# Sorted-block attention and a routed expert layer on one core: expert 0's last output as seven products, and part of a weight sum on another engine

## Chip, core and metric

The kernel runs on one core of a Trainium2 chip. The core has TensorE (matrix products into PSUM), VectorE, ScalarE and GpSimd (elementwise work), SyncE (it issues DMAs here) and 16 DMA engines. The metric is the device time of one execution in microseconds (us). Before the change the median of three runs is 681.45 us, and the runs lie between 679.47 and 681.47.

In the profile, PE is TensorE's matmuls, PEld its weight loads, DVE VectorE, ACT ScalarE, POOL GpSimd. L305 is line 305 of the kernel.

## What is computed

Four batches of 768 tokens with 8 heads of 64 go through a block attention whose keys and values are mixed by a small normalised matrix. Its output, 3072 tokens by 512, is the input x of an expert layer in which every expert works on every token, and a routing matrix P weighs the experts:

```python
logits = x @ w_gate                       # 3072 x 8
P = np.exp(logits - logits.max())
for _ in range(8):                        # eight rounds
    P /= P.sum(1, keepdims=True) + 1e-09  # rows: one token's experts
    P /= P.sum(0, keepdims=True) + 1e-09  # columns: one expert's tokens
    P *= N / E
for e in range(8):
    h = np.maximum(x @ w1[e], 0.0)        # 512 -> 1024
    out += P[:, e:e+1] * (h @ w2[e])      # 1024 -> 512
```

P is final only after eight rounds over all tokens, so it needs the attention of the last batch. The expert products do not need it; only the weighing of their outputs does.

## The kernel before

**Layout.** Matmul operands are bf16. `xtT` holds x transposed (features on partitions, 4 blocks of 128), `osbl` the output in f32 as 24 tiles of 128 tokens by 512, `glog` the logits and later P, 24 x 8 per partition. `w1t[e]` and `w2t[e]` are an expert's weights.

**Stages.** (1) Attention of batch 0, then of batches 1 to 3 with expert 0's products for batches 0 and 1 woven in. (2) Routing (`balance`, L440 to L476) with expert 0's products for batches 2 and 3 (`last_two`, L625), and, from the second of these batches on, with expert 1's first hidden units. (3) Experts 1 to 7, each for three groups of 1024 tokens: while one group's hidden layer is made (`hidden`, L481), the output of the group before it is made (`output7`, L559).

**Expert 0** uses plain products. `hidden0` makes 384 tokens' hidden layer in 8 steps of 4 matmuls of 384 columns (L305), with ReLU on ScalarE (L307). `output0` makes one tile of 128 tokens with 8 matmuls of 512 columns (L314) in two half steps; ScalarE then copies it to `osbl` (`keep`, L322) or, for batch 3, multiplies it by P's column as it copies (`keep_scaled`, L325), for which the rounds must be over.

**Experts 1 to 7** use seven products of half-size blocks in place of eight. That needs sums of operands: of x on VectorE (`sum_x`, L139, three plus one in place for each group of 1024 tokens), of w1 and w2 on GpSimd (`sum_w`, L338; `sum_w2`, L437) and of the hidden layer on GpSimd (`sum_h`, L557). A `hidden` unit has seven steps of two 512-column matmuls (L487). Between them ScalarE copies partial results out of PSUM (L507, L515, L520, L529) and VectorE adds them (L511, L523, L526, L533). Step 0's result is copied and then accumulated further in step 2, so step 2 waits for the copy. `output7` has seven steps of four 256-column matmuls (L574), each followed by a VectorE multiply-add into `osbl` (`gather`, L539). `scale0` (L609) multiplies expert 0's first 18 tiles by P on ScalarE.

**Routing.** `balance` is a chain. The maximum of the logits goes VectorE (L446), TensorE (L449), VectorE (L451), TensorE (L454), VectorE (L456), ScalarE's exponential (L457). Then eight rounds: VectorE's row steps (L464 to L468), a TensorE matmul that sums over partitions (L471), VectorE's column steps (L472 to L475). Each `yield` is a place at which the caller lets other work in.

**What sets the order.** Each engine runs its instructions in the order of its queue. A scheduler fills the queues from the order of the code and from what it takes to be ready, and moves ready work forward into gaps. `pin` (`keep_in_program_order`) holds an instruction behind all that was traced on its engine before it. The matmuls of stage 2 are pinned, as are the weight sums and weight loads of GpSimd. VectorE's and ScalarE's work and `sum_h` are not.

The last part of the kernel interleaves by hand: loop step `n` issues one step of `last_two`, from n = 28 one step of expert 1's first units, at the steps in `works` one of `sum_x`, and at 19 listed steps the next part of `balance`. At n = 40, behind the last round, a small GpSimd copy of P into `held` (L652) stands ahead of the eight sums for expert 1's w2, so they start only when routing is done. `load_w2(1)` is issued as soon as the attention's buffers are closed.

Of the kernel before, what the change touches and what calls it, by code (L numbers as in the profile page):

```python
# [13 lines left out]
F32 = mybir.dt.float32  # L14
BF16 = mybir.dt.bfloat16
AF = mybir.ActivationFunctionType
AX = mybir.AxisListType
ALU = mybir.AluOpType


def mkap(t, dims, off=0):
    return bass.AP(tensor=t.tensor, offset=t.offset + off, ap=dims)
# [3 lines left out]
def kernel(  # L26
# [11 lines left out]
    nc = tc.nc  # L38
    B, H, S, D = 4, 8, 768, 64
    NB, BL = 8, 96  # L40
    N, Dm, E, F = 3072, 512, 8, 1024
    NT = 24
    TB = S // 128
    scale = 1.0 / (D ** 0.5)
# [19 lines left out]
    pin = tc.keep_in_program_order  # L64
# [12 lines left out]
    w2t = {}  # L77
# [6 lines left out]
    def load_w2(e):  # L84
        w2t[e] = (wq if e else wcp).tile([128, 8, Dm], BF16, name="w2e")
        pin(nc.gpsimd.dma_start(out=w2t[e],
                                in_=moe_w2[e].rearrange("(fb k) f -> k fb f", k=128)))
# [18 lines left out]
    cs = pp.tile([32, 8], F32)  # L106
# [21 lines left out]
    osbl = xtp.tile([128, NT, Dm], F32)  # L128
    glog = xtp.tile([128, NT, E], F32)
# [168 lines left out]
            yield  # L298


    def hidden0(c0, hTs, hbank):
        for fb in range(8):
            hps = hbank()
            for kk in range(4):
                pin(nc.tensor.matmul(hps[:, 0:384], w1t[0][:, kk, fb * 128:(fb + 1) * 128],  # L305
                                     xtT[:, kk, c0:c0 + 384], start=(kk == 0), stop=(kk == 3)))
            nc.scalar.activation(out=hTs[:, fb, 0:384], in_=hps[:, 0:384], func=AF.Relu)  # L307
            yield

    def output0(c0, hTs, obank, done):  # L310
        for tt in range(3):
            oacc = obank()
            for fb in range(8):
                pin(nc.tensor.matmul(oacc, hTs[:, fb, tt * 128:(tt + 1) * 128],  # L314
                                     w2t[0][:, fb, :], start=(fb == 0), stop=(fb == 7)))
                if fb == 3:
                    yield
            done(c0 // 128 + tt, oacc)
            yield

    def keep(t, oacc):
        (nc.vector.tensor_copy if t < 12 else nc.scalar.copy)(osbl[:, t, :], oacc)  # L322

    def keep_scaled(t, oacc):
        nc.scalar.activation(out=osbl[:, t, :], in_=oacc, func=AF.Copy,  # L325
                             scale=glog[:, t, 0:1])

    wct = {}

# [11 lines left out]
    with tc.tile_pool(name="ps0", bufs=8, space=bass.MemoryType.PSUM,  # L341
# [14 lines left out]
        held = pp.tile([96, 2], BF16)  # L356
# [18 lines left out]
    with ExitStack() as c2:  # L375
# [13 lines left out]
        for bb, ns in ((1, (5, 3, 3, 5)), (2, (5, 3, 2, 4)), (3, (5, 4, 0, 5))):  # L389
# [11 lines left out]
            else:  # L401
                for _ in sums:
                    pass
                x0 = sum_x(0)
# [3 lines left out]
        for _ in ex:  # L408
# [6 lines left out]
    mpc, xcp, wq, wcq = late("mpc", 1), late("xcp", 2), late("wq", 2), late("wcq", 1)  # L415
    htp, fsp, hsp, w2q = late("htp", 2), late("fsp", 1), late("hsp", 3), late("w2q", 1)
# [2 lines left out]
                                        reuse_waits="tile"))  # L419
    op = ctx.enter_context(tc.tile_pool(name="op", bufs=3, space=bass.MemoryType.PSUM,  # L420
                                        reuse_waits="tile"))
    load_w2(1)

    def bank():
        return bk.tile([128, 512], F32, name="bk")

    w2s = {}

    def sum_w2(e):
        w2s[e] = (w2q.tile([128, 4, 4, Dm // 2], BF16, name="w2s") if e % 2 else  # L430
                  wcp.tile([128, 4, 4, Dm // 2], BF16, name="w2e"))
        for k in (0, 2):
            b11, b12 = (w2t[e][:, 4 + k:6 + k, d:d + 256] for d in (0, 256))
            b21, b22 = (w2t[e][:, k:k + 2, d:d + 256] for d in (0, 256))
            t1, t2, t3, t4 = (w2s[e][:, j, k:k + 2, :] for j in range(4))
            for a, b, c in ((b12, b11, t1), (b22, t1, t2), (b22, b12, t3), (b21, t2, t4)):
                pin(nc.gpsimd.tensor_tensor(out=c, in0=a, in1=b, op=ALU.subtract))  # L437
                yield

    def balance():  # L440
        onesc = mpc.tile([128, 128], F32)
        nc.vector.memset(onesc, 1.0)
        I128 = mpc.tile([128, 128], F32)
        nc.vector.tensor_copy(I128, Ibig)
        gm = mpc.tile([128, 1], F32)
        nc.vector.reduce_max(out=gm, in_=glog.rearrange("p t e -> p (t e)"), axis=AX.X)  # L446
        yield
        gmps = bank()[:, 0:128]
        pin(nc.tensor.matmul(gmps[0:1, :], gm, I128, start=True, stop=True))  # L449
        gm1 = mpc.tile([1, 1], F32)  # L450
        nc.vector.reduce_max(out=gm1, in_=gmps[0:1, :], axis=AX.X, negate=True)  # L451
        yield
        gnps = bank()[:, 0:128]
        pin(nc.tensor.matmul(gnps[:, 0:1], onesc[0:1, :], gm1, start=True, stop=True))  # L454
        gneg = mpc.tile([128, 1], F32)
        nc.vector.tensor_copy(gneg, gnps[:, 0:1])  # L456
        nc.scalar.activation(out=glog, in_=glog, func=AF.Exp, bias=gneg)  # L457

        rs2 = mpc.tile([128, NT], F32)
        cs2 = mpc.tile([128, E], F32)  # L460
        cs1 = mpc.tile([128, E], F32)
        yield
        for it in range(8):
            nc.vector.reduce_sum(out=rs2, in_=glog, axis=AX.X)  # L464
            nc.vector.tensor_scalar_add(rs2, rs2, 1e-9)
            nc.vector.reciprocal(out=rs2, in_=rs2)
            nc.vector.tensor_mul(glog, glog, mkap(rs2, [rs2.ap[0], rs2.ap[1], [0, E]]))
            nc.vector.reduce_sum(out=cs2, in_=glog.rearrange("p t e -> p e t"), axis=AX.X)  # L468
            yield
            csps = bank()[:, 0:128]  # L470
            pin(nc.tensor.matmul(csps[:, 0:E], onesc, cs2, start=True, stop=True))  # L471
            nc.vector.tensor_scalar(out=cs1, in0=csps[:, 0:E], scalar1=float(E) / N,  # L472
                                    scalar2=1e-9 * E / N, op0=ALU.mult, op1=ALU.add)
            nc.vector.reciprocal(out=cs1, in_=cs1)
            nc.vector.tensor_mul(glog, glog, mkap(cs1, [cs1.ap[0], [0, NT], cs1.ap[1]]))  # L475
            yield  # L476
# [60 lines left out]
    def gather(e, t, c, ps):  # L537
        o = osbl[:, t, c:c + ps.shape[-1]]
        nc.vector.scalar_tensor_tensor(out=o, in0=ps, scalar=glog[:, t, e:e + 1], in1=o,  # L539
                                       op0=ALU.mult, op1=ALU.add)  # L540
# [5 lines left out]
    hs = {}  # L546

    def sum_h(i, hT, f0=0, f1=4):

        if f0 == 0:  # L550
            hs[i] = hsp.tile([128, 3, 4, 128], BF16, name="hs")
        s1, s2, s4 = (hs[i][:, j, f0:f1] for j in range(3))
        a11, a21, a12, a22 = (hT[:, f + f0:f + f1, t + 128 * i:t + 128 * i + 128]
                              for f in (4, 0) for t in (0, 512))
        for a, b, o, c in ((a21, a22, ALU.add, s1), (s1, a11, ALU.subtract, s2),
                           (a12, s2, ALU.subtract, s4)):
            nc.gpsimd.tensor_tensor(out=c, in0=a, in1=b, op=o)  # L557
# [54 lines left out]
    def units(e, p, hT, hold=lambda ins: ins):  # L612
        for i in range(4):
            yield from hidden(e, p, i, hT, hold)

    queue = [sum_w2(1)]

    def sums(n):
        while n and queue:
            if next(queue[0], 0) is None:  # L620
                n -= 1
            else:
                queue.pop(0)

    def last_two():  # L625
        for bb, done in ((2, keep), (3, keep_scaled)):
            hT = htp.tile([128, 8, 1024], BF16, name="hT")
            halves = [(bb * S + c, hT[:, :, c:c + 384]) for c in (0, 384)]
            for c0, hTs in halves:
                yield from hidden0(c0, hTs, bank)  # L630
            for c0, hTs in halves:
                yield from output0(c0, hTs, lambda: op.tile([128, Dm], F32, name="oacc"), done)

    tail0, chain = last_two(), balance()
    x1, x2 = sum_x(1), sum_x(2)
    works = {0: x0, 10: x1, 14: x1, 19: x1, 23: x1, 41: x2, 43: x2, 46: x2, 48: x2}
    first = None
    for n in range(56):
        next(tail0)
        if n == 28:  # L640
            hT = htp.tile([128, 8, 1024], BF16, name="hT")
            first = units(1, 0, hT, pin)
        if first:
            next(first)
            if n == 28 + 21:
                sum_h(0, hT, 0, 3)
        if n in works:
            next(works[n], 0)
        if n in (0, 2, 4, 6, 8, 11, 13, 15, 17, 20, 22, 24, 26, 29, 31, 33, 35, 37, 39):
            next(chain)  # L650
        if n == 40:
            pin(nc.gpsimd.tensor_copy(held, glog[0:96, NT - 1, 0:2]))  # L652
            sums(8)

    hTs = {0: hT}

# [8 lines left out]
    for n in range(1, 3 * (E - 1) + 1):  # L665
        e, p, hT = 1 + (n - 1) // 3, (n - 1) % 3, hTs[n - 1]
        d = 2 + n // 3
# [49 lines left out]
```

## Time and profile before

| | |
|---|---|
| median of 3 runs | 681.45 us |
| profiled execution | 680.18 us, span 678.2 us |
| TensorE busy | 651.5 us, 96% of the span |
| VectorE, GpSimd, ScalarE busy | 545.2, 472.6, 298.5 us |
| routing: first row step to end of last column step | 120.31 to 153.35 us |
| TensorE's first matmul of `output7` | 172.51 us |

The profile's page has a row of busy tenths in 40 slices of the span (about 17 us each), the chain of work that ended last as shares of the span, and groups of instructions by line. The trace behind it gives every instruction with its start and length in us, then engine, line, operation and tiles; the number in brackets is how long the engine was idle before it and what ended that wait. Rows of waits give the engine and line that waited, what it waited for, the total, the times and the longest.

### The profile page before, as it was taken

Reading aid. Unit: us, or ns where it says so; the run is one execution under the profiler, and the core shown is the slowest. Engines: PE = TensorE matmul, PEld = TensorE weight load, DVE = VectorE, ACT = ScalarE, POOL = GpSimd, SP = SyncE. Lnnn points to the kernel's source line nnn. Section 1 sums busy time; section 2 is a strip of 40 time slices with the busy share of each in tenths; the row PEclk is TensorE's granted clock in tenths of the full one; section 3 lists DMA queues with packets and bytes.
Section 4 is the critical chain, followed back from the end, with each engine's and each line's share of the span. In section 5 each row is a group of like instructions: output and inputs, shape, how many; then the busy total and the mean of one; then the engine's idle time right before and its main releaser. Section 6 shows DMA issues by size and latency. Waiting matters only on the chain.

```text
span 678.2 us, 13166 instructions
## 1 busy us (share of the span) xinstructions
PE 651.5 (96%) x5033; PEld 436.5 (64%) x5108; DVE 545.2 (80%) x1154; ACT 298.5 (44%) x550; POOL 472.6 (70%) x499
## 2 busy tenths in 40 slices
PE   2999999999999999999999999999999999999996
PEld 1756766554566666666666666666666666666675
DVE  6727768763788888888988889888888889888896
ACT  3747764469533433334333343434333343333430
POOL 4542335007888988898997898689886999646745
PEclk9789999999999999999999999999999999999999
DMA  9898973100240330030303040034003120001223
GB/s 146 164 218 127 150 125 46 31 1 12 52 61 3 63 60 5 1 63 4 61 1 47 17 63 1 1 63 63 1 2 63 19 45 0 1 1 64 94 78 141
DMA packets 31903, 36.57 MB, mean 54 GB/s; under 512 B 2016, under 2 KB 24288, under 8 KB 31840
## 3 DMA queue, kind: packets, MB, share of 16 engines
q0 software_dynamic: 26400, 27.82, 25.9%
q1 hardware_dynamic: 5440, 7.90, 3.6%
q8 instruction: 40, 0.66, 0.4%
q14 instruction: 23, 0.19, 0.1%
HBM read 52.45 MB, written 6.29 MB: 87 GB/s over the span
## 4 chain that ended last, share of the span: by engine, by line
PE 72%; DVE 1%; issue 1%; POOL 1%; ACT 0%; DVEq 0%
PE oacc L574 37%; PE bk L487 34%; PE bk L574 1%; DVE osbl L539 1%; POOL hs L557 1%; DVE hT L523 0%; DVE hT L526 0%; ACT p L507 0%; DVEq L539 0%
## 5 line engine op out<-in xcount | busy, mean ns | idle before, releaser
L539 DVE SCALAR_TENSOR_TENSOR osbl<-oacc,glog,osbl 128x256 f32<-128x256 f32 (+1 forms) x490 | 255.7, 522 | 61.4 <-PE oacc L574 61.3
L557 POOL TENSOR_TENSOR hs<-hT 128x512 bf16<-128x512 bf16 (+2 forms) x105 | 99.5, 961 | 67.7 <-DVE hT L526 67.6
L487 PE MATMUL bk<-xtT,w1e 128*128 128x512 bf16 x475 | 143.5, 379 | 0.9
L574 PEld LDWEIGHTS <-hT 128*128 128x128 bf16 x1008 | 98.6, 98 | 64.5 <-issue 1.2
L574 PEld LDWEIGHTS <-hs 128*128 128x128 bf16 x1008 | 98.5, 98 | 64.5 <-POOL hs L557 1.5
L574 PE MATMUL oacc<-w2e,hT 128*128 128x256 bf16 x796 | 119.6, 273 | 1.0 <-ACT hT L529 0.5
L529 ACT ACTIVATE hT<-bk 128x512 bf16<-128x512 f32 x84 | 50.3, 599 | 158.2 <-PE bk L487 140.4
L557 POOL TENSOR_TENSOR hs<-hT,hs 128x512 bf16<-128x512 bf16 (+2 forms) x105 | 99.9, 959 | 4.9
L557 POOL TENSOR_TENSOR hs<-hs,hT 128x512 bf16<-128x512 bf16 (+2 forms) x105 | 100.0, 960 | 4.2 <-ACT hT L529 0.4
L487 PE MATMUL bk<-xc,wc 128*128 128x512 bf16 x319 | 96.3, 379 | 0.6 <-ACT p L507 0.2
L574 PE MATMUL oacc<-w2e,hs 128*128 128x256 bf16 x612 | 92.0, 273 | 1.6 <-POOL hs L557 0.9
L515 ACT COPY u<-bk 128x512 f32<-128x512 f32 x84 | 49.3, 587 | 95.4 <-PE bk L487 82.4
L487 PEld LDWEIGHTS <-w1e 128*128 128x128 bf16 x672 | 65.8, 98 | 10.4
L523 DVE CUSTOM_DVE_ANT_0 hT<-bk,p 128x512 bf16<-128x512 f32 x84 | 58.1, 692 | 11.5 <-ACT p L520 6.4
L533 DVE SCALAR_TENSOR_TENSOR h<-bk,hT 128x512 bf16<-128x512 f32 x84 | 57.2, 681 | 5.8 <-ACT hT L529 5.8
L520 ACT COPY p<-bk 128x512 f32<-128x512 f32 x84 | 49.4, 588 | 23.2 <-PE bk L487 23.2
L507 ACT COPY p<-bk 128x512 f32<-128x512 f32 x84 | 49.4, 588 | 20.3 <-PE bk L487 20.3
L511 DVE CUSTOM_DVE_ANT_0 hT<-bk,p 128x512 bf16<-128x512 f32 x84 | 57.3, 682 | 0.9 <-ACT hT L307 0.5
L526 DVE CUSTOM_DVE_ANT_0 hT<-bk,u 128x512 bf16<-128x512 f32 x84 | 57.2, 680 | 1.0 <-PE bk L487 1.0
L574 PE MATMUL oacc<-w2s,hs 128*128 128x256 bf16 x364 | 54.8, 273 | 0.3
L487 PEld LDWEIGHTS <-wc 128*128 128x128 bf16 x504 | 49.3, 98 | 8.0 <-issue 0.4
L487 PE MATMUL bk<-xc,w1e 128*128 128x512 bf16 x159 | 48.0, 379 | 0.0
(116 smaller groups left out, 834.9 us busy)
## 6 DMA issues: line engine op xcount, KB each, us to landing
w1e<-in_moe_w_dram POOLq DMA_DIRECT2D x8, 1024.0 KB, 8.2
w2e<-in_moe_w_dram POOLq DMA_DIRECT2D x8, 1024.0 KB, 8.9
out_dram<-osbl SPq DMA_DIRECT2D x23, 256.0 KB, 2.0
kvq<-in_v_dram POOLq DMA_DIRECT2D x3, 768.0 KB, 10.4
vsb<-vs SPq DMA_DIRECT2D x16, 97.5 KB, 4.3
vsb<-vs POOLq DMA_DIRECT2D x16, 97.5 KB, 3.9
kvq<-in_q_dram POOLq DMA_DIRECT2D x4, 384.0 KB, 12.9
kvq<-in_k_dram POOLq DMA_DIRECT2D x4, 384.0 KB, 13.5
```

The costliest lines, as they stand in the source:

```text
L487: hold(nc.tensor.matmul(ps, wa[:, kk, :], xa[:, kk, :], start=(first and kk == 0), stop=(kk == 1), skip_group_check=True))
L507: nc.scalar.copy(p1, u)
L511: nc.vector._custom_dve(TENSOR_ADD_SAT, out=c11, in0=w, in1=p1, s0=TOP, s1=0.0)
L515: nc.scalar.copy(u2, u)
L520: nc.scalar.copy(p5, v)
L523: nc.vector._custom_dve(TENSOR_ADD_SAT, out=c22, in0=u, in1=p5, s0=TOP, s1=0.0)
L526: nc.vector._custom_dve(TENSOR_ADD_SAT, out=c12, in0=v, in1=u2, s0=TOP, s1=0.0)
L529: nc.scalar.activation(out=c21, in_=u, func=AF.Relu)
L533: nc.vector.scalar_tensor_tensor(out=h3[e, p][:, i, :], in0=u, scalar=0.0, in1=c22, op0=ALU.max, op1=ALU.subtract)
L539: nc.vector.scalar_tensor_tensor(out=o, in0=ps, scalar=glog[:, t, e:e + 1], in1=o, op0=ALU.mult, op1=ALU.add)
L557: nc.gpsimd.tensor_tensor(out=c, in0=a, in1=b, op=o)
L574: nc.tensor.matmul(ps, h[:, fb, :], w[:, fb, :], start=(first and fb == 0), stop=(fb == 3), skip_group_check=True)
```

## The change

For batch 3, `output0` and `keep_scaled` are replaced by seven products for pairs of token tiles: tile 18 + i with 21 + i, i = 0, 1, 2.

- `sum_w2_0` makes four sums of expert 0's w2 blocks in eight GpSimd instructions, pinned, in a second buffer of the pool that holds `w2t[1]`. `load_w2(1)` is issued behind them.
- `hidden0` takes its 8 blocks in the order 0, 4, 1, 5, ... and calls back after each.
- `sum_h0` makes the hidden sums of a pair, four GpSimd instructions, pinned; the first pair's in two halves while the last hidden blocks are still being made.
- `pair0` makes the seven products of a pair, four 256-column matmuls each. Four parts of the result are multiplied by P and written by ScalarE (`put`), two are added by VectorE (`gather`).
- The loop is split. 44 steps issue batch 2 and batch 3's hidden layer with all the rounds, spread anew. Then 28 steps issue expert 1's first units and, in between, the 21 products of the pairs.
- Four of the eight sums for expert 1's w2 go to VectorE, not pinned. The `held` copy (its use at L652) is gone.

```diff
-    def hidden0(c0, hTs, hbank):
-        for fb in range(8):
+    def hidden0(c0, hTs, hbank, each=lambda n: None):
+        for n, fb in enumerate((0, 4, 1, 5, 2, 6, 3, 7)):
...
+            each(n)
             yield
...
-    load_w2(1)
-
...
             for a, b, c in ((b12, b11, t1), (b22, t1, t2), (b22, b12, t3), (b21, t2, t4)):
-                pin(nc.gpsimd.tensor_tensor(out=c, in0=a, in1=b, op=ALU.subtract))
+                if e == 1 and k:
+                    nc.vector.tensor_tensor(out=c, in0=a, in1=b, op=ALU.subtract)
+                else:
+                    pin(nc.gpsimd.tensor_tensor(out=c, in0=a, in1=b, op=ALU.subtract))
                 yield
...
+    def sum_w2_0():
+        w2s[0] = wq.tile([128, 4, 4, Dm // 2], BF16, name="w2e")
+        for k in (0, 2):
...
+            for a, b, c in ((b12, b11, t1), (b22, t1, t2), (b22, b12, t3), (b21, t2, t4)):
+                pin(nc.gpsimd.tensor_tensor(out=c, in0=a, in1=b, op=ALU.subtract))
+
+    def sum_h0(i, hA, hB, f0=0, f1=4):
...
+        for a, b, o, c in ((a21, a22, ALU.add, s1), (s1, a11, ALU.subtract, s2),
+                           (a11, a21, ALU.subtract, a21), (a12, s2, ALU.subtract, s4)):
+            pin(nc.gpsimd.tensor_tensor(out=c, in0=a, in1=b, op=o))
+
+    def pair0(i, hA, hB):
+        a, b = 18 + i, 21 + i
...
+        def put(t, c, ps):
+            nc.scalar.activation(out=osbl[:, t, c:c + 256], in_=ps, func=AF.Copy,
+                                 scale=glog[:, t, 0:1])
...
+        add(u, hA[:, 4:8, cs], b11, True)
+        put(a, 0, u)
+        yield
+        add(x0, hA[:, 0:4, cs], b21, True)
+        yield
+        add(x1, s1, t1, True)
+        put(b, 256, x1)
+        yield
+        add(u, s2, t2, False)
+        put(a, 256, u)
+        yield
+        add(x1, s4, b22, False)
+        gather(0, a, 0, x)
+        yield
+        add(u, s3, t3, False)
+        gather(0, b, 256, u)
+        yield
+        add(u, hB[:, 0:4, cs], t4, False)
+        put(b, 0, u)
+        yield
+
+    def pairs0(hA, hB):
+        p = [pair0(i, hA, hB) for i in range(3)]
+        for i in (0, 0, 0, 0, 0, 1, 0, 1, 0, 1, 1, 1, 2, 1, 2, 1, 2, 2, 2, 2, 2):
+            next(p[i])
+            yield
...
+    sum_w2_0()
+    load_w2(1)
     tail0, chain = last_two(), balance()
     x1, x2 = sum_x(1), sum_x(2)
-    works = {0: x0, 10: x1, 14: x1, 19: x1, 23: x1, 41: x2, 43: x2, 46: x2, 48: x2}
+    works = {0: x0, 11: x1, 17: x1, 21: x1, 25: x1, 47: x2, 51: x2, 55: x2, 59: x2}
+    rounds = (0, 2, 4, 6, 9, 10, 15, 16, 19, 20, 23, 24, 27, 28, 33, 34, 38, 39, 43)
+    for n in range(44):
         next(tail0)
...
+        if n in rounds:
             next(chain)
+    hT = htp.tile([128, 8, 1024], BF16, name="hT")
+    first, n = units(1, 0, hT, pin), 0
+    for m in range(28):
+        next(first)
+        if m == 5:
             sums(8)
+        if m == 20:
+            sum_h(0, hT, 0, 3)
+        while n * 28 < (m + 1) * 21:
+            next(tail0)
+            n += 1
```

## Prediction

> **What bounds the kernel now.** I read the page's slices first, then the chain that ended last, then busy time by stretches of 6 us, then who TensorE waits for, then the timeline of the stretch that the change touches.
>
> ```profile
> PE   2999999999999999999999999999999999999996
> ```
>
> ```profile
> PE 72%; DVE 1%; issue 1%; POOL 1%; ACT 0%; DVEq 0%
> PE oacc L574 37%; PE bk L487 34%; PE bk L574 1%; DVE osbl L539 1%; POOL hs L557 1%; DVE hT L523 0%; DVE hT L526 0%; ACT p L507 0%; DVEq L539 0%
> ```
>
> TensorE is full in every slice but the first and last, and the chain is its matmuls. So from about 20 us on a microsecond that TensorE loses or saves anywhere arrives at the end whole, and work on another engine counts only if TensorE waits for it. The stretches (columns: PE, PEld, DVE, ACT, POOL busy):
>
> ```profile
> 114.00:120.00 6.00, 5.72 (x35) 3.03 (x34) 5.11 (x13) 2.64 (x6) 0.18 (x1) 1.00 0.95 128
> 120.00:126.00 6.00, 5.53 (x37) 3.32 (x36) 4.11 (x14) 4.10 (x10) 0.00 (x0) 1.00 0.29 49
> 156.00:162.00 6.00, 5.95 (x29) 2.71 (x28) 2.36 (x4) 6.00 (x12) 5.92 (x5) 1.00 0.00 0
> 168.00:174.00 6.00, 5.30 (x27) 2.36 (x26) 1.89 (x3) 5.94 (x11) 2.66 (x4) 1.00 1.00 173
> ```
>
> TensorE loses 0.3 and 0.5 us where routing begins and 0.7 at 168:174. GpSimd does nothing through the rounds (the `held` copy, L652, waits 39.2 us for the last of them). ScalarE is 100% busy from 156 to 174, because the 18 scalings of L609 fill every gap it has. Who TensorE waits for from 100 to 200 us:
>
> ```profile
> PE bk L471 <- DVE cs L468: 0.7, 2, 0.5
> PE oacc L574 <- ACT hT L529: 0.5, 1, 0.5
> PE bk L454 <- DVE gm L451: 0.3, 1, 0.3
> PE bk L487 <- ACT p L507: 0.2, 1, 0.2
> ```
>
> From 175 us to the end it waits under 2 us in all. So the change can win its saved matmul columns and these waits, and it can lose by new waits.
>
> **Seven products, -1.25 us.** Batch 3's output was 6 tiles of 8 matmuls with 512 columns. Back to back, two 512-column matmuls take 0.43 us in the chain of waits and four 256-column ones 0.44 (0.87 for the pair of rows), so 0.216 and 0.109 each. Old: 48 x 0.216 = 10.37. New: 3 pairs x 7 products x 4 x 0.1086 = 9.12. All on the path.
>
> **Expert 0's weight sums at the head of the routing, +6.3 us.** Eight GpSimd subtractions of 1.15 us (L437's row) now stand directly behind GpSimd's last L338, which ends at 113.25 us, where the load of w2 for expert 1 was issued. The timeline there:
>
> ```profile
> 115.84 1.28 DVE L139 TENSOR_TENSOR xc<-xtT 128x1024 bf16<-128x1024 bf16 x2
> ...
> 118.24 0.27 DVE L451 TENSOR_REDUCE gm<-bk 1x1 f32<-1x128 f32 x1
> 118.44 1.27 DVE L139 TENSOR_TENSOR xc<-xtT,xc 128x1024 bf16<-128x1024 bf16 x2
> 118.66 0.35 PE L454 MATMUL bk<-gm,onesc 1*128 1x1 f32 x2 [0.28 <-DVE gm L451]
> ```
>
> VectorE runs six sums of x (L139, 0.64 us from start to start) around the two small maximum steps of the routing, L446 and L451. Its rows follow one another in the order issued, so the routing stands behind them, and TensorE waits at L454 and at round 1. The code sends those sums later, but they are not held in program order and their inputs are ready, so I expect them in the same place. GpSimd was idle then. Before has one place where an L139 and an L437 meet:
>
> ```profile
> 154.79 1.16 POOL L437 TENSOR_TENSOR w2s<-w2e,w2s 128x512 bf16<-128x512 bf16 x1
> 155.61 0.89 DVE L139 TENSOR_TENSOR xtT<-xtT 128x1024 bf16<-128x1024 bf16 x1
> 155.91 1.61 POOL L437 TENSOR_TENSOR w2s<-w2e 128x512 bf16<-128x512 bf16 x1
> 157.47 1.16 POOL L437 TENSOR_TENSOR w2s<-w2e,w2s 128x512 bf16<-128x512 bf16 x1
> ```
>
> The L139 took 0.89 instead of 0.68 and began 0.3 before a GpSimd subtraction ended; the next subtraction took 1.61 instead of 1.16. Together they lost 0.66 us, about one whole L139: they took turns. No other L437 of the run is above 1.17, and none of those meets a VectorE instruction with both inputs in SBUF. If they take turns all along: subtraction 3 ends at 116.7, so the first L139 waits 0.86; L139s 2, 3, 4 each wait a whole subtraction (3 x 1.15); L451 runs beside one, so the fifth waits 0.88; the sixth 1.15. Sum 6.3. Bounds: nothing if the sums stand elsewhere, 6 x 0.21 = 1.3 by the one lengthened row taken as a flat price, 6.3 by turns. I take 6.3, since the two rows together show turns and here both queues are full.
>
> The Trainium skill (SBUF — State Buffer, Who interferes with whom) says that VectorE and GpSimd share one port pair under an exclusive lock, and that an instruction with two SBUF inputs blocks one of GpSimd that reads SBUF, or is blocked by it, until the first has finished. By that rule the sum is the 6.3 of turns; by the lengthened L139 alone it would be 1.3. The two rows agree with the rule.
>
> **The rounds, -0.95 and +0.35.** Round 1's column matmul (L471, at 122.19 with 0.47 of wait) stands one hidden step later, so 4 x 0.162 = 0.65 us of matmuls now fill part of that wait. The later rounds lie at least 5 x 0.65 + 0.14 = 3.4 us apart on TensorE; a round takes 3.14 (L468's end at 122.13, next at 125.27), so they add nothing, and the 0.3 that round 3 lost goes. The last round meets GpSimd's sums of the first pair, which begin 2 us before it ends (0.6 us each, between the 0.42 and 0.92 of L557's rows for 128 and 384 columns): L467 and L475 have two SBUF inputs, half a sum each, 0.6 less the 0.25 of slack: +0.35 (0 to 0.9).
>
> **Pairs beside expert 1's first units, +2.0 us.** Before, a unit step (0.43) alternated with a hidden step or half an output tile (0.65 to 0.86), so from the matmuls of one step to those of the next but one, which need what ScalarE copied between, 2.2 to 2.6 us passed. Now 28 unit steps and 21 products alternate: 1.73, or 1.30 where two unit steps follow each other. Needed: 0.59 for the matmuls, 0.09 until ScalarE starts (180.06 to 180.74), 0.59 for the copy, 0.05 back: 1.32. The 18 scalings still come when glog is final, so ScalarE is full again (units 9.5 us, 12 partial copies of about 0.45, an estimate from L457's 0.45 for 192 columns, scalings 12.6, in 21 us), and a copy finds an instruction ahead of it. The row that stopped TensorE at 173.5 shows such a copy late: L529 starts at 172.78, about 1 us after its matmuls. Six of twelve copies fall on the short distance: 6 x 0.3 = 1.8. Two VectorE sums on it need 1.42: 0.2. The last pair's product 7 follows product 6 after 0.87 but needs L539's read (0.60 + 0.1 + 0.47): 0.35. In all 2.4, of which TensorE's own pauses give ScalarE back some: 2.0 (0.5 with ScalarE on time, 4.5 with 0.7 late each). The 0.7 lost at 168:174 stays: unit 27 is still last before output7. Between 156 and 168 us the same full ScalarE cost TensorE 0.1, because the distances were long; that is the cover that goes.
>
> GpSimd itself is in time: with 0.7 + 11.8 us for the pairs' sums after the last hidden block, 4.6 for its half of expert 1's w2 sums and 2.7 for sum_h it is done about 20 us into 21. Its four sums on VectorE cost 4 x 0.35 (half an L139 each) beside some 16 of 21 us: nothing, unless they stand ahead of the rounds (rival 3). load_w1(2) is issued a few us later and is needed by sums that are queued behind other work for 10 us.
>
> **Sum.** 6.3 - 1.25 - 0.95 + 0.35 + 2.0 = +6.45 us, on the profiled execution's 680.18 us (span 678.2): 686.6. The median of the runs shown is 681.45, their spread 2 us; about 0.3% (2 us) is what this kernel's measurement can tell from no change.
>
> **Rivals.** (1) *The head stays clear.* The scheduler puts the x sums behind the routing's steps, where VectorE waits for TensorE anyway. Then 6.3 becomes about 0.3: 680.18 + 0.45 = 680.6 (679.5 to 683). For it: their place in the code has moved back. Against: it was already far behind where they ran. Chance 0.24. (2) *Faster: the waits go.* As (1), and ScalarE's scalings spread over the following stage, whose rows show it under 40% busy, so that the copies are on time and both the 0.7 us at 168:174 and the 1.0 for L471 and L454 vanish: 680.18 - 1.25 - 0.7 - 1.0 = 677.2. It decides if L507 to L529 start within 0.1 us of their matmuls. Chance 0.10. (3) *VectorE waits for w2.* The load that was issued at 113.25 now goes after eight subtractions and five turns, 113.25 + 9.2 + 3.2 = 125.7, and lands 8.9 later (its row) at 134.6. The four VectorE sums are not pinned; ordered right behind round 1's row steps (128.8) they would hold VectorE 5.8 us, less 0.9 of slack before round 2: 691.5. Against: they may as well stand after it has landed. Chance 0.14. (4) *The pause lowers the clock.* TensorE would wait 4.5 us at L454; the page shows grants of 0.66 to 0.69 between 25 and 40 us, where 32 hidden matmuls took 7.04 us, 0.22 each. Twenty at half clock are 3.2 us more, 2.1 of them hidden in round 1's wait: 687.7. Chance 0.07, inside the forecast's range.
>
> The Trainium skill (TensorE: Matmul & The Clock Gate, Part 1) has the clock halve after an idle window of about 3.4 us, so it would make rival 4 likelier than this trace does, which shows no such pause between matmuls at full grant.
>
> **Numbers.** Forecast 0.45 (683.5 to 690 alone), rivals 0.24, 0.10, 0.14, 0.07. The range 679.5 to 692 leaves out most of (2) and the end of (3). Slower by over 0.3%: forecast, (3), (4) and a little of (1): 0.68. Within: 0.22. Faster: 0.10.
>
> **What would show it.** L139s of 1.5 us or more between 115 and 127 us beside lengthened L437s; TensorE's wait for gm up from 0.3 to about 4.5; no wait at later rounds above 0.5; TensorE waits for ScalarE's p and u in the 21 us of pairs, 2 us in all; then the same steady stage. If the L139s are at 0.68 each, the largest term is wrong. If VectorE idles for the w2 load inside the rounds, rival 3 holds.

## The result and the profile after

The changed kernel takes 698.28 us (median of 5 runs, 697.76 to 700.3), the kernel before 680.15 (5 runs): a ratio of 1.0266, 95% interval 1.0244 to 1.0289. It is 18 us slower. The forecast was 686.6 and its range ended at 692.

The page of the changed kernel, TensorE's row and its granted clock in 40 slices of 17.5 us:

```profile
PE   2999997399999999999999999999999999999997
PEclk9779999599999999999999999999999999999999
```

The seventh and eighth slices hold the loss: TensorE is busy for three tenths of the eighth, and its clock is halved there. The same place in stretches of 6 us (PE, PEld, DVE, ACT, POOL busy, then the clock, the DMA share and GB/s):

```profile
114.00:120.00 6.00, 3.80 (x44) 2.17 (x42) 1.02 (x2) 0.98 (x2) 5.92 (x7) 1.00 0.00 0
120.00:126.00 6.00, 0.00 (x0) 0.00 (x0) 0.00 (x0) 0.00 (x0) 5.07 (x5) 0.56 0.01 1
126.00:132.00 6.00, 0.00 (x0) 0.00 (x0) 0.00 (x0) 0.00 (x0) 0.00 (x0) 0.50 1.16 167
132.00:138.00 6.00, 3.63 (x12) 1.32 (x12) 4.87 (x13) 0.66 (x2) 0.00 (x0) 0.50 0.04 6
138.00:144.00 6.00, 6.00 (x30) 3.34 (x29) 3.46 (x11) 3.41 (x8) 0.00 (x0) 0.73 0.01 3
```

From 118 to 133 us TensorE, VectorE and ScalarE all stand still; first only GpSimd works, then only a DMA. The timeline of the changed kernel names each (L632 is `sum_w2_0`, L86 the load of expert 1's w2, L433 its four VectorE sums, L270 the copy of the last batch's logits, L305 the hidden layer):

```profile
115.13 9.13 POOL L632 TENSOR_TENSOR w2e<-w2e 128x512 bf16<-128x512 bf16 x8
...
124.20 0.94 POOL L86 DMA_DIRECT2D w2e<-in_moe_w_dram  x1
133.13 0.42 DVE L433 TENSOR_TENSOR w2s<-w2e 128x512 bf16<-128x512 bf16 x1 [18.11 <-DMA w2e<-in_moe_w_dram]
133.47 0.20 DVE L270 COPY glog<-bank 128x48 f32<-128x48 f32 x1
...
133.72 1.44 PE L305 MATMUL bk<-xtT,w1e 128*128 128x384 bf16 x4 [15.92 <-DVE glog L270]
...
135.67 1.28 DVE L139 TENSOR_TENSOR xc<-xtT 128x1024 bf16<-128x1024 bf16 x2
```

Read it from TensorE's row (L305) upwards. TensorE waited 15.92 us for the 0.2 us logits copy, which has to empty a PSUM bank. The copy stood in VectorE's queue behind the first L433. That one waited 18.11 us for the w2 load, and the load was issued at 124.2, behind GpSimd's eight sums. The x sums (L139) then ran at 0.64 us from start to start, because GpSimd was done: the turns of the forecast did not happen here at all.

The profiled runs reach the last logits matmuls at unequal times, before first, then after:

```profile
113.54 0.29 PE L266 MATMUL bank<-wg,xtT 128*128 128x8 bf16 x6
```

```profile
115.32 0.29 PE L266 MATMUL bank<-wg,xtT 128*128 128x8 bf16 x6
```

To compare them I count from there to the end of the span: before 678.2 - 113.54 = 564.7 us, after 698.2 - 115.32 = 582.9, so 18.2 more. TensorE's wait is 15.9 of it. The clock was half until about 141.2 (0.50, then 0.73 over a stretch of 6 us). TensorE worked for 6.9 us of the time from 133.7 to there, and did 3.4 us of work less than at full clock. A wait of 0.7 for the maximum is new, and the waits of before's routing, 1.0 in all, are gone. That leaves about -0.8 for the rest of the change.

### The profile page after: what moved, and what is told of

It reads as the page before. It is cut to its first block, busy times and chain, and to the rows that moved or that the text cites. A ratio compares the mean times of both kernels' runs of the same rounds, so it can differ in the third digit from the quotient of the medians.

```text
span 698.2 us, 13359 instructions
## 1 busy us (share of the span) xinstructions
PE 660.3 (95%) x5144; PEld 441.6 (63%) x5144; DVE 542.2 (78%) x1164; ACT 299.3 (43%) x556; POOL 490.6 (70%) x518
## 4 chain that ended last, share of the span: by engine, by line
PE 71%; POOL 1%; DVE 1%; ACT 1%; issue 0%; POOLq 0%; ACTq 0%; DVEq 0%
PE bk L485 36%; PE oacc L572 35%; POOL hs L555 1%; PE oacc L655 1%; DVE osbl L537 0%; DVE hT L521 0%; ACT osbl L607 0%; PE bk L572 0%; POOLq L794 0%; ACT u L513 0%; DVE hT L524 0%; ACT osbl L659 0%; ACT p L505 0%; ACT p L518 0%; ACTq L513 0%
## 5 line engine op out<-in xcount | busy, mean ns | idle before, releaser
L537 DVE SCALAR_TENSOR_TENSOR osbl<-oacc,glog,osbl 128x256 f32<-128x256 f32 (+1 forms) x496 | 251.6, 521 | 64.0 <-PE oacc L572 62.2
L485 PE MATMUL bk<-xtT,w1e 128*128 128x512 bf16 x504 | 162.7, 378 | 0.6 <-ACT u L513 0.5
L485 PE MATMUL bk<-xc,wc 128*128 128x512 bf16 x336 | 99.9, 379 | 0.3 <-ACT p L505 0.3
L485 PE MATMUL bk<-xc,w1e 128*128 128x512 bf16 x168 | 50.0, 379 | 0.1
```

The lines of the kernel that those rows point to most:

```text
L485: hold(nc.tensor.matmul(ps, wa[:, kk, :], xa[:, kk, :], start=(first and kk == 0), stop=(kk == 1), skip_group_check=True))
```

## The experiments

"Before" stands for the runs of the kernel before on the same chip, 680.1 to 680.4 us in each group. The last column is TensorE's longest waits in the stage.

| kernel | us | ratio to before (95%) | TensorE waited for |
|---|---|---|---|
| after | 698.28 | 1.0266 (1.0244 to 1.0289) | logits copy 15.9 |
| e1_pin | 688.82 | 1.0118 (1.0104 to 1.0132) | gm 4.1, osbl 2.5 |
| e2_pool | 686.34 | 1.0091 (1.0076 to 1.0105) | gm 4.2, hs 2.2 |
| e3_load_first | 689.86 | 1.0139 (1.0124 to 1.0154) | logits copy 6.9, gm 1.5 |
| e4_dve_alone | 690.03 | 1.0139 (1.0124 to 1.0155) | logits copy 7.2 |
| e5_xpin | 683.43 | 1.0048 (1.0034 to 1.0061) | osbl 3.0 |
| e6_gated | 681.99 | 1.0028 (1.0016 to 1.0040) | rounds 1.8, u and p 1.0 |
| e7_gated_scale | 680.24 | 0.9998 (0.9989 to 1.0006) | rounds 1.8 |
| e8_head_sums | 686.13 | 1.0086 (1.0072 to 1.0100) | gm 3.8, rounds 0.8 |
| e9_before_scale | 679.63 | 0.9992 (0.9983 to 1.0002) | rounds 0.7 |
| e10_apart | 678.61 | 0.9975 (0.9965 to 0.9985) | rounds 0.5 |

**The stop.** Three kernels part the place in VectorE's queue from the place of the load.

e1_pin:

```diff
-                    nc.vector.tensor_tensor(out=c, in0=a, in1=b, op=ALU.subtract)
+                    pin(nc.vector.tensor_tensor(out=c, in0=a, in1=b, op=ALU.subtract))
```

> The changed kernel with its four VectorE sums of expert 1's w2 held behind all that is traced on VectorE before them, so that they no longer stand ahead of the logits copy. Theory A (the whole loss is VectorE's wait for the load, 15.9 us of TensorE, and the halved clock behind it, some 3.5): both go, and what is left is the rest of the change, 698.3 - 15.9 - 3.5 = 679, within 0.3% of before. Theory B (the forecast's own terms also hold: GpSimd's eight sums and VectorE's six sums of x take turns at the head of the routing, 6.3 us, and the pairs lose 2.0 to ScalarE): about 686.6, with the L139s at 1.5 us or more.

Theory B came out, 2 us above its number. The wait for the logits copy is gone, and the turns appear. Timeline of e1_pin (line numbers as in after; L449 and L452 are the maximum steps that were L451 and L454):

```profile
113.63 11.29 POOL L632 TENSOR_TENSOR w2e<-w2e 128x512 bf16<-128x512 bf16 x8
...
116.28 2.95 DVE L139 TENSOR_TENSOR xc<-xtT 128x1024 bf16<-128x1024 bf16 x2
...
122.69 0.55 PE L452 MATMUL bk<-gm,onesc 1*128 1x1 f32 x2 [4.10 <-DVE gm L449]
123.17 6.15 PE L305 MATMUL bk<-xtT,w1e 128*128 128x384 bf16 x20
```

GpSimd's eight sums took 11.29 us here against 9.13 in after, where VectorE stood; two L139s took 2.95 against 1.28. TensorE waited 4.1 us for the maximum, and the 20 matmuls behind the pause took 0.31 us each; the next 24, at full clock again, took 0.17 each.

e3_load_first exchanges two lines, so that the load is issued first:

```diff
-    sum_w2_0()
     load_w2(1)
+    sum_w2_0()
```

> The changed kernel with the load of expert 1's w2 issued ahead of GpSimd's eight sums instead of behind them. Theory A: VectorE's queue still has the sums ahead of the logits copy, but the load lands about 9 us earlier (issue near 115, 9.8 to landing), so VectorE waits until about 125 instead of 133 and TensorE about 7.7 us: near 690, a little less if the clock drops for a shorter time. Rival (the load's place in GpSimd's queue is the whole cause): 679 to 681.

689.86: as Theory A said. e4_dve_alone is the kernel before with the change's lines for L433 and nothing else:

```diff
+                if e == 1 and k:
+                    nc.vector.tensor_tensor(out=c, in0=a, in1=b, op=ALU.subtract)
+                else:
+                    pin(nc.gpsimd.tensor_tensor(out=c, in0=a, in1=b, op=ALU.subtract))
```

> The kernel before with only the second half of the change: four of expert 1's eight w2 sums on VectorE, not held in order; the load stays where it was, issued at 113.25 us, landing near 122. Theory A: VectorE stands from about 113 to 122 ahead of the logits copy and TensorE waits 6 to 7 us, plus 2 to 3 for a lowered clock: 688 to 690. Rival (only the later load does harm): 680.

690.03. The timeline of e4_dve_alone (L438 are its VectorE sums) shows after's stop on a smaller scale:

```profile
123.23 0.43 DVE L438 TENSOR_TENSOR w2s<-w2e 128x512 bf16<-128x512 bf16 x1 [9.37 <-DMA w2e<-in_moe_w_dram]
...
123.82 1.44 PE L305 MATMUL bk<-xtT,w1e 128*128 128x384 bf16 x4 [7.19 <-DVE glog L270]
```

So the cause is the place in VectorE's queue; the load's place only sets how long TensorE stops (7 us with the load early, 16 us with it late). The four small sums, with nothing else changed, cost 9.7 us. Why the scheduler put them ahead of the logits copy, which the code issues long before them, no run shows; that it takes the load to land sooner than it does is argued only.

**The moved sums, once they do not block.** e2_pool gives all eight sums back to GpSimd:

```diff
-                if e == 1 and k:
-                    nc.vector.tensor_tensor(out=c, in0=a, in1=b, op=ALU.subtract)
-                else:
-                    pin(nc.gpsimd.tensor_tensor(out=c, in0=a, in1=b, op=ALU.subtract))
+                pin(nc.gpsimd.tensor_tensor(out=c, in0=a, in1=b, op=ALU.subtract))
```

> The changed kernel with all eight sums of expert 1's w2 on GpSimd: the second half of the change undone. Theory A: no wait of VectorE for the load, and GpSimd has 4 x 1.15 = 4.6 us more ahead of the first sums of expert 1's hidden layer, which were just in time; so e1_pin's time plus 1 to 3 us. Theory B: the same step above a higher e1_pin, 688 to 690. If the moved half is worth nothing where it does not block, the two are equal.

It was faster than e1_pin by 2.5 us, where both theories had it slower or equal. GpSimd was late as expected (2.2 us of wait for `hs`), but e1_pin lost more. Its timeline in the pairs (L643 is `sum_h0`, L655 the pairs' matmuls):

```profile
162.69 1.37 DVE L433 TENSOR_TENSOR w2s<-w2e 128x512 bf16<-128x512 bf16 x1
...
163.74 1.34 POOL L643 TENSOR_TENSOR hs<-hT 128x512 bf16<-128x512 bf16 x1
163.99 1.38 DVE L433 TENSOR_TENSOR w2s<-w2e,w2s 128x512 bf16<-128x512 bf16 x1
...
167.01 0.60 PE L655 MATMUL oacc<-w2e,hT 128*128 128x256 bf16 x4 [2.54 <-DVE osbl L537]
```

The sums take turns with GpSimd's pair sums, 1.38 us instead of 0.42, and a multiply-add behind them reaches TensorE 2.5 us late. By the profiled runs, counted as above, e1_pin is only 1.0 us longer than e2_pool. Another 1.1 lies ahead of the logits (113.75 us against 112.67), in a stage that the two edits leave alone. Why it differs there stays open, so 1.0 is the safer price of the moved half.

**The turns at the head.** e8_head_sums adds only `sum_w2_0` and the late load to the kernel before. e5_xpin is e1_pin with the sums of x held in later rounds:

```diff
-            nc.vector.tensor_tensor(out=c, in0=a, in1=b, op=ALU.subtract)
+            (pin if p else lambda ins: ins)(
+                nc.vector.tensor_tensor(out=c, in0=a, in1=b, op=ALU.subtract))
             yield
...
-    works = {0: x0, 11: x1, 17: x1, 21: x1, 25: x1, 47: x2, 51: x2, 55: x2, 59: x2}
+    works = {0: x0, 11: x1, 17: x1, 21: x1, 25: x1, 29: x2, 31: x2, 35: x2, 47: x2}
```

> The kernel before with one thing added: the eight GpSimd sums of expert 0's w2 (their result is not used) at the head, and load_w2(1) behind them, as in the change. Turns: the six x sums at 1.5 us instead of 0.68, TensorE's wait for gm 4 us, round 1 some 6.5 us later; 680.3 + 6.3, plus 1 to 2 for the clock behind the pause: 686.5 to 688.5. Rival (GpSimd's work beside the routing is free, and e1_pin's loss is from the pairs): 680 to 681.

> e1_pin with VectorE's sums of x for groups 1 and 2 also held where the code sends them (group 1 at steps 11, 17, 21, 25; group 2 at 29, 31, 35, 47), so that none of them stands at the head of the routing while GpSimd runs its eight sums. Turns at the head cost 6.3 us and the pause some clock: TensorE's wait for gm falls from 4.1 to under 0.5, and the time from 688.8 to about 682 to 683.5 (the seven x sums inside the rounds exceed their slack by some 1.4 us; the 2.5 us wait in the pairs stays). Rival (GpSimd's sums slow the routing's own small steps as much, whoever takes turns): 687 or more.

e8 was 5.8 us slower than before, just under its range: L139's median is 1.53 us against 0.68, and the copy ahead of the exponential ends at 125.16 us against 119.78, 5.4 later (e8 first, then before):

```profile
125.01 0.15 DVE L454 COPY gneg<-bk 128x1 f32<-128x1 f32 x1
```

```profile
119.64 0.14 DVE L456 COPY gneg<-bk 128x1 f32<-128x1 f32 x1
```

e5 was 5.4 us faster than e1 and has no wait for gm. Putting the turns in costs what taking them out gives back. e5's wait of 3.0 us in the pairs stayed, as said.

**ScalarE beside the pairs.** e6_gated keeps the seven products and is meant to set the GpSimd and VectorE sums apart. The load is first again. In each of the first seven rounds one of GpSimd's eight sums for expert 0 (two in round 2) follows a small copy that waits for the row steps. VectorE's four sums, now the first half in the code, are held behind the row steps of rounds 3 and 6. The main lines:

```diff
             nc.vector.reduce_sum(out=cs2, in_=glog.rearrange("p t e -> p e t"), axis=AX.X)
+            pin(nc.gpsimd.tensor_copy(held[:, 0:1], cs2[0:96, 0:1]))
+            for _ in range((1, 2, 1, 1, 1, 1, 1, 0)[it]):
+                next(w20)
             yield
...
+        if n in (16, 28):
+            sums(2)
```

e7_gated_scale is e6 with `pin` on L609's scalings, which so run two at a time in the output stage.

> The changed kernel with every turn avoided: load_w2(1) first as before; GpSimd's eight sums of expert 0's w2 one by one (two in round 2) behind each round's row steps, while VectorE waits for TensorE; expert 1's four VectorE sums held behind the row steps of rounds 3 and 6. The seven products alone: 680.3 - 1.25 - 0.95 + about 0.7 for the last round and the pairs' waits seen in e1_pin (0.5 and 0.5 against 0.7 before): 678.5 to 679.5. Rival (the pairs lose 2.0 to ScalarE, as forecast): 680 to 681.

> e6_gated with the 18 scalings held where the code sends them, two ahead of each output block of expert 1, so that none fills ScalarE beside the pairs. If full ScalarE costs the pairs 2.0 us: 2 us below e6_gated. If it costs under 0.5, as the waits of e1_pin say: equal within 0.5, since a few tenths may come back as waits in the output stage.

e6 came out above both of its ranges, at 681.99, and e7 1.75 us below it, near what the forecast had set for full ScalarE. The stretch from 150 us, e6 first, then e7:

```profile
150.00:156.00 6.00, 4.88 (x33) 2.88 (x31) 3.37 (x8) 4.64 (x10) 5.84 (x9) 1.00 0.00 0
```

```profile
150.00:156.00 6.00, 5.62 (x39) 3.57 (x38) 4.34 (x9) 3.58 (x8) 5.84 (x9) 1.00 0.00 0
```

With scalings in the gaps TensorE loses 1.1 us of these six, without them 0.4. The rest of e6's surplus is in the rounds. Waits of e7 (L472 is the column matmul of a round):

```profile
PE bk L472 <- DVE cs L466: 1.1, 3, 0.5
PE bk L472 <- ACT osbl L323: 0.7, 1, 0.7
```

In rounds 3 and 6 a VectorE sum and a GpSimd sum had been put behind the same row steps and met; the timeline of e7 in round 3, where an L433 took 1.40 us instead of 0.42:

```profile
130.94 1.14 POOL L635 TENSOR_TENSOR w2e<-w2e 128x512 bf16<-128x512 bf16 x1
130.97 1.40 DVE L433 TENSOR_TENSOR w2s<-w2e,w2s 128x512 bf16<-128x512 bf16 x1
```

**Everything apart.** e10_apart issues GpSimd's sums two at a time behind rounds 1, 4, 5 and 7 only, `if it in (0, 3, 4, 6)`, where VectorE has none. e9_before_scale is the kernel before with the held scalings alone.

> The kernel before with only its 18 scalings held where the code sends them. In before they filled ScalarE up to 174 us and the one cost seen was TensorE's 0.5 and 0.2 us behind L529 and L507 at the start of output7: 0.7 us less, 679.6. If the scalings then make the output stage's copies late, equal or slower. What e7_gated_scale owes to this part alone is read from it: if e9 is 0.7 below before, the seven products with everything set apart are worth nothing net.

> e7_gated_scale with GpSimd's eight sums in pairs behind the row steps of rounds 1, 4, 5 and 7, none in the rounds in which VectorE has a sum of its own (2, 3 and 6). In e7 TensorE waited 1.8 us for late rounds, where an L433 or L139 met a GpSimd sum. If those meetings are the cause, about 1.0 to 1.5 us less than e7: 679.0. If two sums in one round delay its column steps as much as the meetings did, equal to e7.

e9: 679.63, 0.5 us below before, with an interval that includes no change; TensorE's waits of 0.5 and 0.2 for L529 and L507 are gone. So of the 1.75 between e6 and e7 about 0.5 may be no price of the pairs: the kernel before seems to pay it too. e10: 678.61, faster than before by 1.5 us (0.15 to 0.35%) and than e7 by 1.6. Its L433s are back at 0.42 us, and TensorE's waits in its rounds are down from 1.8 to 0.5. This is the version that beats both kernels. Less e9's part, the seven products with all that they need are worth about 1.0 us.

## Why the prediction was wrong

**The reading of the bound was right, the direction was luck.** TensorE's lost time arrives at the end whole: 15.9 us of wait and the halved clock make up the 18. But the forecast called the change slower for its 6.3 us of turns, and by its own sign that term failed here: in after the L139s take 0.68 us each, and TensorE's waits for `gm` are 0.7 in all. The kernel is slower for another reason.

**The step that failed** is the sentence that the four sums on VectorE cost "nothing, unless they stand ahead of the rounds (rival 3)". They stood ahead of them, and not where rival 3 put them. Rival 3 had the mechanism, the late landing (134.6 forecast, 133.1 seen) and a chance of 0.14, but it set the sums behind round 1's row steps, at 128.8 us, and priced 4.9 (5.8 less 0.9 of slack). They stood in front of the last logits copy, where VectorE had nothing left to do from 115.0 on, ahead of every step of the routing. So VectorE stood for 18.1 us and TensorE for 15.9. A bound from both sides for an instruction that is not held would have had to run from the moment its buffer is free, 113 us, to the landing: about 20 us, and the range would have reached 700.

**The stop also took the turns away.** Rival 3 added its stop to the 6.3 us of turns, which fits the place where it set the sums. Where they really stood the two exclude each other: while VectorE stands, GpSimd finishes alone.

**Turns at the head, 6.3 us:** right in kind; absent in after, and 5.4 to 5.8 in e8 and e5 once the stop is gone. e1_pin, the change without the stop, took 688.8 where the forecast had 686.6. The two rows from which the turns were read were enough.

**Pairs beside full ScalarE, 2.0 us:** right in kind and somewhat high in size: 1.75 between e6 and e7, or about 1.2 without the 0.5 that e9 gains with no pairs at all, inside the stated 0.5 to 4.5. In after itself TensorE's waits for `u` and `p` are 0.8.

**Seven products, -1.25, and rounds, -0.95:** e10 less e9 is -1.0, with some waits left in its rounds; no run parts the two terms.

**GpSimd in time:** right for the half (e1_pin waits 0.2 us for `hs` in all), and the other half is what it could not have taken (2.2 us in e2). But that VectorE would take its half for nothing was wrong a second time: held beside the pairs, the sums meet GpSimd's, and e1_pin is slower than e2.

**Rival 4, the clock:** its chance of 0.07 was too low: the clock fell in after and in e1, e2, e3, e4, e5 and e8, every kernel in which TensorE waited 3 us or more behind the logits. Its 1.1 us fits e1_pin, where round 1's row steps end at 127.9 us but its matmul starts at 129.16, behind the slow hidden matmuls.

## What to carry to other kernels

When work that reads a load is moved to an engine's queue and nothing holds its place, look for what it could stand in front of, and price the move at the whole time from the freeing of the buffer to the landing. Before a sum is moved from GpSimd to VectorE, or placed on GpSimd beside VectorE, look for instructions on the other one with two SBUF inputs at that time: here the two took turns (1.38 us instead of 0.42 for a moved sum), so the second engine gained little. A gain of about 1 us needed five placements to come through (e10): the VectorE sums behind the load, the same sums away from the pairs, GpSimd's sums away from the head, the two kinds of sums in different rounds, and the scalings out of the gaps. Each one missed cost about as much as the gain or more.

## What the hardware showed beyond expectation

Read in stretches of 0.1 us, TensorE's granted clock in these runs is 1.00 or 0.50, and only the stretch of a change lies between. When it fell and came back, in us:

| kernel | TensorE stood | clock fell | clock back | time at half |
|---|---|---|---|---|
| after | 117.8 to 133.7 | 120.8 | 141.3 | 20.5 |
| e4_dve_alone | 116.6 to 123.8 | 121.8 | 132.1 | 10.3 |
| e3_load_first | 116.6 to 123.5 | 119.4 | 129.6 | 10.2 |
| e2_pool | 117.5 to 121.7 | 120.2 | 127.0 | 6.8 |
| e1_pin | 118.6 to 122.7 | 121.9 | 128.8 | 6.8 |
| e8_head_sums | 118.5 to 122.3 | 122.4 | 125.8 | 3.4 |
| e5_xpin | 158.4 to 161.5 | 161.2 | 164.7 | 3.4 |

Every time at half clock is 3.4 us or a whole multiple of it. In the last 3.4 us of each, TensorE was busy for 3.2 us or more; in the 3.4 us before that, where there was one, for 2.8 at most (after and e4). So what a stop costs beyond its own length seems to depend on where its end falls in this grid. In e8 TensorE went on as the clock fell and was at half for 3.4 us; in e1 it went on 0.8 us later, was busy for 2.7 of the next 3.4 us, and was at half for 6.8. A wait of 3.0 us (e5) was enough for the fall; waits of 2.5 (e1_pin, in the pairs) and 2.2 (e2_pool, behind them) left the clock at 1.00. How idle TensorE must be is not shown: in before the clock also fell at 26.7 and 36.9 us, for 6.8 and 3.4 us, with no wait above 1.1 us between 16 us and there.

The Trainium skill (TensorE: Matmul & The Clock Gate, Part 1) has the clock fall after an idle window of about 3.4 us and return after a busy one. It adds that the window runs freely and does not restart when the kernel starts. The times at half clock agree with both; that a wait of 3.0 us, shorter than a window, is enough is what e5 measured.

Two full queues of instructions with two SBUF inputs each did not slow each other evenly: in e8 and e1 VectorE's L139 went from 0.68 to 1.53 us, GpSimd's sum from 1.14 to 1.41.
